# The last query pair as seven block products, early output sums in the wait, and split LayerNorm statistics, in a two-layer linear-attention and gated-MLP kernel

## The chip, the cores and the metric

The kernel runs on one core of one Trainium2 chip. The metric is the time on the device in microseconds (us). All runs that the comparisons below use are in the fast state, at a granted TensorE clock of 1.00 wherever a profile shows it.

## The reference, cut to what matters

```python
q, k, v = split(layernorm(x) @ wqkv)          # 2048 tokens, 1024 wide, 32 heads of 32
pq, pk = phi(q), phi(k)                       # phi(t) = t + 1 if t > 0 else exp(t), plus 1e-6
kv = einsum("bhsd,bhse->bhde", pk, v)
z = sum of pk over the tokens
o = (pq @ kv) / (pq . z + 1e-6)
x = x + o @ wo                                # block A
x = x + ((layernorm(x) @ w_gate) * (layernorm(x) @ w_up)) @ w_down    # block B
# A, B, A, B with the same weights
```

## The kernel before

Block A passes through four stages. First, the projections. Most of them are **quads**: two tiles of 128 tokens, and both halves of the output columns, by a Strassen-Winograd scheme of seven block products (28 matmuls of 512 columns where plain projections take 32). Then the kernel sums over the tokens (`g_part`, `kvt`), a mask keeps the diagonal blocks of heads, and these are multiplied with `wo` (`wprod`). This gives one matrix `wp`. Last comes the output loop, `x + xnT @ wp`, tile by tile. VectorE makes the LayerNorm statistics of the next block in between.

Between the sum and the output loop there is a chain: last `kvt` on TensorE, mask on VectorE, `wprod` on TensorE, evacuation (finished sums are copied out of a **bank**, one of the buffers of PSUM, `ps` in the profile, that the matmuls fill), output. Before the change, two query tiles were held back from the quads to fill it with plain projections:

```python
items += [("k", 6), ("k", 7), ("q", 6)]            # the quad ("q", 7) is missing
...
ph = proj("q", *held[0])            # 8 matmuls each
kvt(2 * KT - 1)
ph()
proj("q", *held[1])()
for g in range(4, 8):
    wprod(g, [0, 4, 1, 3][g - 4], g % 2 == 0)
proj("q", *held[2])()
for g in range(4, 8):
    wprod(NG + g, [0, 2, 1, 3][g - 4], g % 2 == 0)
proj("q", *held[3])()
```

The quads of layer two carry the LayerNorm statistics of the last four tiles, each in one piece:

```python
job(n, 0, lnp.flush_b)
if n % 2:
    job(n, 2, lnp.flush_a)          # two bn_stats and one aggregate, on VectorE
```

And at the end of the output loop of layer one, this work on VectorE prepares block B.

```python
if first and i >= 14:
    prep_s(i - 14)                  # four weight sums of a gate or up unit
...
if nxt.t_next >= 8 and RG["tq"] is None:
    RG["tq"] = t_ops(0)             # block differences; the first reads transposed tiles up to 7
for _ in range(2 if i > 12 else 1):
    if RG["tq"]:
        RG["tq"].pop(0)()
```

Of the kernel before, what the change touches and what calls it, by code (L numbers as in the profile page):

```python
# [180 lines left out]
def build_kernel(nc, A_x, A_wqkv, A_wo, B_w_gate, B_w_up, B_w_down, out):  # L181
    _, S, D = A_x.shape
    F = B_w_gate.shape[1]
    NST, NSB, KT, NG, NFT, NDH = S // 128, S // 512, D // 128, D // 128, F // 128, D // 512
# [8 lines left out]
    NHOLD = 2  # L193
# [52 lines left out]
    O_WP = RA  # L246
# [79 lines left out]
    with ExitStack() as es:  # L326
# [56 lines left out]
        def psb(b):  # L383
            return ps[:, b, :]
# [5 lines left out]
        B_TP = 3  # L390
        B_G = [0, 4]
        B_KVT = [1, 2]
        B_Z = [5, 6]
        B_YY = [5, 6, 7, 3]
        B_GX = [0, 1]
        B_GY = [2, 3]
# [12 lines left out]
        def R(o, n):  # L409
            return [(o, o + n)]  # L410

        def r_x(i, lo=0, hi=D):
            return [(O_X + (i * D + lo) * 2, O_X + (i * D + hi) * 2)]
# [7 lines left out]
        def r_xT(s0, s1):  # L421
            return _seg(O_XT, KT, S * 2, s0 * 2, s1 * 2)

        def r_w(base, lo, hi):
            return _seg(base, KT, D * 2, lo * 2, hi * 2)
# [22 lines left out]

        ln_cnt = [0]

        def ln_a(i, mid=None):
            j = ln_cnt[0] % 8
            ln_cnt[0] += 1
            for h in range(2):
                P.add("dve", (lambda h: lambda e: e.bn_stats(st[j][:, 6 * h:6 * h + 6], x_res[:, i, (D // 2) * h:(D // 2) * (h + 1)]))(h),  # L455
                      rd=r_x(i, (D // 2) * h, (D // 2) * (h + 1)), wr=R(O_ST[j] + 24 * h, 24))
                if mid and h == 0:
                    mid()
            P.add("dve", lambda e: e.bn_aggr(mv[j][:, 0:2], st[j]), rd=R(O_ST[j], 48), wr=R(O_MV[j], 8))
            P.add("pool", lambda e: e.tensor_scalar(out=mv[j][:, 2:3], in0=mv[j][:, 1:2], scalar1=EPS_LN, scalar2=None, op0=ALU.add),  # L460
                  rd=R(O_MV[j] + 4, 4), wr=R(O_MV[j] + 8, 4))
            ln_rstd(j)
            return j
# [36 lines left out]
        class LN:  # L500

            def __init__(self, to, order):
                self.to = to
                self.order = order
                self.q_b = []
                self.q_s = []
                self.q_n = []
                self.q_t = []
                self.n = 0
                self.t_next = 0  # L510
                self.use_dma = False
                self.on_act = False

# [110 lines left out]
                    self.b1_one()  # L624
                    self.b2_one()

            def flush_a(self):
                if self.n < NST and self.pending_ab() < 3:
                    self.start(self.n)

            def flush_step(self):
                self.step_t(1)
# [277 lines left out]
        def layer_A(lnp, nxt, first):  # L910
# [46 lines left out]
            class Quad:  # L957
                n = 0

                def __init__(self, kind, p):  # L960
                    n = Quad.n
                    Quad.n += 1
                    self.kind, self.p = kind, p
                    self.X, self.Z, self.Y = QX[n % 2], QZ[n % 2], QY[(n + NPL) % 3]
                    self.u2 = (u2sb[n % 2], R(O_U2[n % 2], 2048))
                    self.u3 = (u3sb, R(O_U3, 2048))
                    self.i, self.i2 = tok[2 * p], tok[2 * p + 1]
# [208 lines left out]
            for p in range(npr, 6):  # L1176
                items += [("k", p), ("q", p)]
            if npr < 8:
                items += [("k", 6), ("k", 7), ("q", 6)]
            jobs = {}  # L1180

            def job(n, j, f):
                jobs.setdefault((n, j), []).append(f)
# [9 lines left out]
            for n, (kind, p) in enumerate(items):  # L1193
                if kind == "k" and n:
                    sm = s_make(tok, p)
                    job(n - 1, 1, lambda p=p: lnp.need(2 * p + 1))
                    job(n - 1, 1, sm[0])
                    job(n - 1, 2, sm[1])
                    job(n - 1, 3, sm[2])
                    job(n, 1, sm[3])  # L1200
                if kind == "k" and not first:
                    for t in (tok[2 * p], tok[2 * p + 1]):
                        job(n, 0, lambda t=t: dma(xrt[t], nscr[t * 128:(t + 1) * 128, :], r_xr(t), KNL[t], rd=R(V_XN + t * 32, 32)))
                if first:
                    i = NPL + len(LNX) + n
                    for j in range(2):
                        if i < NST:
                            job(n, 2 * j, lambda i=i, j=j: lnstep(i, j))
                    c, m = 9 - max(NPL - 3, 0), len(items)
                    if (n + 1) * c // m > n * c // m:  # L1210
                        job(n, 3, pack)
                elif n >= 2:
                    if n == 9:
                        job(n, 0, lambda: rl.update(o=O_XN[0]))
                    job(n, 0, lnp.flush_b)
                    if n % 2:
                        job(n, 2, lnp.flush_a)

            if items:
                job(len(items) - 1, 3, lambda: load_v(0))  # L1220
# [5 lines left out]
                g_part(0, j)  # L1226

            QL = [Quad(kind, p) for kind, p in items]
            held = [(tok[i], h) for i in range(NST - NHOLD, NST) for h in range(2)]

            def g_part(n, j):
                h, jj = n // KT, n % KT
# [55 lines left out]
            def wprod(n, bank, on_act):  # L1288
# [7 lines left out]
                else:  # L1296
                    P.add("dve", lambda e: e.tensor_scalar(out=dst, in0=psb(bank), scalar1=rz[:, g:g + 1], scalar2=None, op0=ALU.mult),
                          prd=[bank], rd=R(O_RZ, 32), wr=wr)

            for n in range(2 * KT):  # L1300
                if n:
                    gchunk(n)
                if first and n % 2 == 0:
                    pack()
                if n == 2:
                    z_final()
                if n == 4:
                    z_col()
                if n >= 1:
                    kvt(n - 1)  # L1310
                if n >= KT + 2:
                    m = n - KT - 2
                    for d in range(2):
                        if m < 4:
                            wprod(d * NG + m, B_Z[d], True)
                if n >= 2 and na[0] < NNORM:
                    norm(tok[na[0]])
                    na[0] += 1
            ph = proj("q", *held[0])
            kvt(2 * KT - 1)  # L1320
            ph()
            proj("q", *held[1])()
            for g in range(4, 8):
                wprod(g, [0, 4, 1, 3][g - 4], g % 2 == 0)
            proj("q", *held[2])()
            for g in range(4, 8):
                wprod(NG + g, [0, 2, 1, 3][g - 4], g % 2 == 0)
            proj("q", *held[3])()

            def y_seed(n):  # L1330
                if n < NST:
                    xs, bank = x_res[:, tok[n], 512:1024], B_YY[(2 * n + 1) % 4]
                    P.add("act", lambda e: e.copy(psb(bank), xs), rd=r_x(tok[n], 512, 1024), pwr=[bank])

            def y_grp(i, dh, n):
                bank = B_YY[(2 * n + dh) % 4]

                def fn(e):
                    return [e.matmul(psb(bank), xnT[:, g, i * 128:(i + 1) * 128], wp[:, g, dh * 512:(dh + 1) * 512],  # L1339
                                     start=(dh == 0 and g == 0), stop=(g == NG - 1), skip_group_check=True) for g in range(NG)]  # L1340
                xs = x_res[:, i, dh * 512:(dh + 1) * 512]
                rx = r_x(i, dh * 512, (dh + 1) * 512)
                P.add("pe", fn, rd=r_xT(i * 128, (i + 1) * 128) + r_w(O_WP, dh * 512, (dh + 1) * 512), pwr=[bank])
                if dh == 0:
                    P.add("dve", lambda e: e.tensor_tensor(out=xs, in0=psb(bank), in1=xs, op=ALU.add), prd=[bank], rd=rx, wr=rx)
                    return
                P.add("act", lambda e: e.copy(xs, psb(bank)), prd=[bank], wr=rx)

            nxt.use_dma = True
            nxt.on_act = YACT  # L1350
            ring_begin(first)
            for _ in range(3):
                ring_issue()
            y_seed(0)
            for i in range(NST):
                if na[0] < NST:
                    if i % 3 == 2:
                        norm(tok[na[0]])
                        na[0] += 1
                elif RG["n"] < NR:  # L1360
                    ring_issue()
                if first and i % 3 == 1:
                    pack()
                nxt.step_t(1)
                nxt.b1_one()
                if 2 <= i < 15:
                    nxt.start(i - 2)
                y_grp(tok[i], 0, i)
                y_seed(i + 1)
                if i < 15:  # L1370
                    nxt.b2_one()
                y_grp(tok[i], 1, i)
                if first and i >= 14:
                    prep_s(i - 14)
                if not first and i >= 8:
                    stash(i - 8)
                if nxt.t_next >= 8 and RG["tq"] is None:
                    RG["tq"] = t_ops(0)
# [3 lines that stand above are left out]
# [691 lines left out]
```

## Time and profile before

| | before |
|---|---|
| median of 3 runs | 1428.89 us (1428.35 to 1429.38) |
| span of the profiled run | 1426.4 us |
| TensorE busy | 99% |
| VectorE busy | 84% |
| ScalarE busy | 51% |

The prediction below shows the lines of the page and of the timeline and how they are read. Two more lines of the page, on the quads: line, engine, operation, shapes, count, then busy us and mean ns, then idle time before.

```profile
L976 PE MATMUL ps<-arena 128*128 128x512 f16 (+1 forms) x605 | 134.0, 379 | 1.2 <-ACT arena L983 0.6
...
L976 PEld LDWEIGHTS ps<-arena 128*128 128x128 f16 x616 | 59.3, 98 | 74.8 <-ACT arena L983 5.9
```

616 is 22 quads of 28; the trace lacks eleven matmul records of these. So a **stop** of TensorE is measured here from the starts of successive matmuls, less 216 ns (less 110 ns for 256 columns, 56 ns for 128), and not from busy time. These are the steps in the trace of before where nothing holds TensorE up: 215 or 216 ns from start to start at 512 columns, 109 or 110 at 256, 55 or 56 at 128.

### The profile page before, as it was taken

What the parts mean: (1) busy time and instruction counts of PE and PEld (TensorE: products, weight loads), DVE (VectorE), ACT (ScalarE), POOL (GpSimd) and SP (SyncE); (2) the same over time, 40 slices, a digit from 0 to 9 for tenths busy, and PEclk for the clock granted to TensorE, in tenths of its full rate; (3) what the DMA queues carried; (4) which work ended last, traced back from release to release, by engine and by line L of the source; (5) the groups of instructions that cost most, each with busy time, mean ns of one, the idle gap of its engine ahead of it and who ended that gap; (6) DMA issues with size and microseconds to landing.
All of it is one profiled execution on the core that took longest, in us unless ns stands there. A gap on an engine that the chain in (4) does not pass through costs nothing.

```text
span 1426.4 us, 21923 instructions
## 1 busy us (share of the span) xinstructions
PE 1417.6 (99%) x8150; PEld 791.0 (55%) x8209; DVE 1200.9 (84%) x2344; ACT 722.0 (51%) x1471; POOL 153.8 (11%) x197
## 2 busy tenths in 40 slices
PE   9999999999999999999999999999999999999999
PEld 4444444555546566664554444456666475666548
DVE  7897978999978799987689978788888877888888
ACT  5882355444420266655377814567776105777400
POOL 3203521000010000002010045310000100000000
PEclk9999999999999999999999999999999999999999
DMA  7868978997786777768884367767775966777553
GB/s 240 218 141 225 216 179 197 310 311 265 252 264 212 234 254 249 252 228 295 239 281 104 92 177 162 172 196 254 258 246 194 329 221 230 259 258 260 191 205 122
DMA packets 270699, 320.74 MB, mean 225 GB/s; under 512 B 164096, under 2 KB 211072, under 8 KB 270592
## 3 DMA queue, kind: packets, MB, share of 16 engines
q1 hardware_dynamic: 270592, 319.34, 73.2%
q8 instruction: 64, 1.05, 0.3%
q14 instruction: 43, 0.35, 0.1%
HBM read 236.45 MB, written 73.40 MB: 217 GB/s over the span
## 4 chain that ended last, share of the span: by engine, by line
PE 92%; DVE 4%; ACT 2%; issue 1%; DMA 1%; POOL 0%; SPq 0%; DVEq 0%
PE ps L1421 29%; PE ps L1504 17%; PE ps L1853 16%; PE ps L1339 8%; PE ps L1237 8%; PE ps L976 8%; PE ps L1760 5%; DVE arena L808 1%; PE ps L949 1%; DVE arena L811 1%; DVE arena L455 1%; ACT arena L668 1%; DMA arena<-in_A_wqkv_dram 1%; PE ps L1263 1%; PE ps L1290 0%
## 5 line engine op out<-in xcount | busy, mean ns | idle before, releaser
L808 DVE TENSOR_TENSOR arena<-arena 128x512 f16<-128x512 f16 (+7 forms) x1027 | 507.3, 522 | 56.9 <-ACT arena L1508 32.7
L1421 PE MATMUL ps<-arena 128*128 128x512 f16 x1888 | 456.8, 379 | 0.1
L811 DVE SCALAR_TENSOR_TENSOR arena<-ps,arena 128x512 f16<-128x512 f32 (+3 forms) x558 | 358.6, 658 | 86.9 <-PE ps L1853 45.0
L1504 PE MATMUL ps<-arena 128*128 128x256 f16 x2184 | 287.5, 273 | 0.1
L1421 PEld LDWEIGHTS ps<-arena 128*128 128x128 f16 (+1 forms) x1888 | 182.9, 98 | 162.4 <-ACT ps L1450 3.8
L1504 PEld LDWEIGHTS ps<-arena 128*128 128x128 f16 (+1 forms) x2184 | 212.3, 98 | 90.4 <-ACT arena L1508 7.2
L1853 PE MATMUL ps<-arena 128*128 128x512 bf16 (+1 forms) x1048 | 230.6, 379 | 0.8
L1853 PEld LDWEIGHTS ps<-arena 128*128 128x128 f16 x1064 | 104.1, 98 | 123.8
L1426 ACT ACTIVATE arena<-ps 128x512 f32<-128x512 f32 x224 | 133.9, 598 | 76.7 <-PE ps L1421 62.5
L1508 ACT ACTIVATE arena<-ps 128x256 f32<-128x256 f32 x351 | 125.1, 384 | 26.4 <-PE ps L1504 21.5
L976 PE MATMUL ps<-arena 128*128 128x512 f16 (+1 forms) x605 | 134.0, 379 | 1.2 <-ACT arena L983 0.6
L1237 PE MATMUL ps<-arena 128*128 128x512 bf16 x498 | 114.7, 379 | 0.7
L1339 PE MATMUL ps<-arena 128*128 128x512 bf16 x502 | 110.3, 379 | 0.5
L1514 ACT COPY ps<-ps 128x256 f32<-128x256 f32 x182 | 66.3, 364 | 75.5 <-DVE arena L811 28.5
L976 PEld LDWEIGHTS ps<-arena 128*128 128x128 f16 x616 | 59.3, 98 | 74.8 <-ACT arena L983 5.9
L1760 PE MATMUL ps<-arena 128*128 128x256 f16 (+1 forms) x882 | 97.0, 273 | 0.0
L1450 ACT COPY ps<-ps 128x512 f32<-128x512 f32 x112 | 65.4, 583 | 61.5 <-PE ps L1421 51.3
L1078 POOL TENSOR_TENSOR arena<-arena 128x1024 f16<-128x1024 f32 x32 | 77.2, 2413 | 155.7 <-DVE arena L1076 140.8
L1760 PEld LDWEIGHTS ps<-arena 128*128 128x128 f16 x882 | 86.2, 98 | 11.0 <-DVE arena L811 0.2
L1517 DVE TENSOR_TENSOR ps<-ps,arena 128x256 f32<-128x256 f32 x182 | 76.7, 428 | 10.7 <-PE ps L1504 9.5
L1339 PEld LDWEIGHTS ps<-arena 128*128 128x128 f16 x512 | 50.1, 98 | 60.4
L1788 ACT COPY arena<-ps 128x256 f32<-128x256 f32 x8 | 3.0, 373 | 155.8 <-PE ps L1760 155.8
(72 smaller groups left out, 981.0 us busy)
## 6 DMA issues: line engine op xcount, KB each, us to landing
arena<-w_scratch SPq DMA_DIRECT2D x84, 896.0 KB, 4.6
arena<-t_scratch SPq DMA_DIRECT2D x32, 896.0 KB, 5.9
arena<-in_B_w_down_dram SPq DMA_DIRECT2D x24, 896.0 KB, 5.0
arena<-sp_scratch SPq DMA_DIRECT2D x26, 768.0 KB, 4.2
w_scratch<-arena SPq DMA_DIRECT2D x28, 512.0 KB, 6.1
arena<-w_scratch SPq DMA_DIRECT2D x28, 384.0 KB, 4.7
x_scratch<-arena SPq DMA_DIRECT2D x40, 256.0 KB, 5.1
arena<-x_scratch SPq DMA_DIRECT2D x40, 256.0 KB, 4.1
```

Source lines behind the costliest of these rows:

```text
L808: P.add("dve", lambda e: e.tensor_tensor(out=out, in0=a, in1=b, op=op), rd=rd, wr=wr, prd=prd)
L811: P.add("dve", lambda e: e.scalar_tensor_tensor(out=out, in0=a, scalar=sc, in1=b, op0=ALU.mult, op1=op1), rd=rd, wr=wr, prd=prd)
L976: P.add("pe", lambda e: [e.matmul(psb(bank), a[0][:, k, :], b[0][:, k, :], start=(q in (1, 5) and k == 0), stop=(k == 3), skip_group_check ...
L1078: P.add("pool", lambda e: e.tensor_tensor(out=asb[b].rearrange("p (h c) -> p h c", c=32), in0=pbuf.rearrange("p (h c) -> p h c", c=32), in ...
L1237: return [e.matmul(psb(bank), xrt[t][:, jj * 128:(jj + 1) * 128], pk[:, h, t, :], start=(t == tok[0]), stop=(t == tok[NST - 1])) for t in ts]
L1339: return [e.matmul(psb(bank), xnT[:, g, i * 128:(i + 1) * 128], wp[:, g, dh * 512:(dh + 1) * 512], start=(dh == 0 and g == 0), stop=(g == ...
L1421: P.add("pe", lambda e: [e.matmul(psb(bank), w[:, k, :], x[:, k, :], start=(start and k == 0), stop=(k == 3), skip_group_check=True) for k ...
L1426: P.add("act", lambda e: e.activation(t, psb(bank), AF.Copy, scale=SG), prd=[bank], wr=r)
L1504: P.add("pe", lambda e: [e.matmul(psb(bank)[:, 256 * half:256 * half + 256], w[:, k, :], xx[:, k, :], start=(start and k == 0), stop=(k == ...
L1508: P.add("act", lambda e: e.activation(d, src, AF.Copy, scale=sc), prd=[xk], wr=rd_)
L1760: P.add("pe", lambda e: [e.matmul(psb(bank)[:, 256 * half:256 * half + 256], a[:, k, 128 * r:128 * r + 128], b[:, k, :], start=(start and ...
L1853: P.add("pe", lambda e: [e.matmul(psb(bank), hv[:, 7 * hf + k, t * 128:(t + 1) * 128], w[:, k, :], start=(q in "15" and hf == 0 and k == 0 ...
```

## The change

The intent is four matmuls fewer per layer. The last query pair becomes a quad. The wait is filled with the first halves of the output sums of tiles 0 and 1, whose `wp` blocks 0 to 3 are ready by then. The statistics are split into two halves in successive quads. Cut to the core:

```diff
-        B_Z = [5, 6]
+        B_Z = [5, 3]
...
-                    self.X, self.Z, self.Y = QX[n % 2], QZ[n % 2], QY[(n + NPL) % 3]
+                    self.X, self.Z, self.Y = QX[n % 2], QZ[n % 2], QY[(n + NPL + 2) % 3]
...
-                items += [("k", 6), ("k", 7), ("q", 6)]
+                items += [("k", 6), ("k", 7), ("q", 6), ("q", 7)]
...
-                    if n % 2:
-                        job(n, 2, lnp.flush_a)
+                    job(n, 2 if n % 2 == 0 else 0, lambda k=int(n % 2 != 0): lnp.flush_a(k))
...
+            y_part(0, 0, 0)
+            y_part(0, 1, 0)
+            kvt(2 * KT - 1)
+            y_part(1, 0, 0)
+            for g in range(4, 8):
+                wprod(g, [0, 1, 4, 2][g - 4], g % 2 == 0)
+            y_part(1, 1, 0)
+            for g in range(4, 8):
+                wprod(NG + g, [0, 1, 4, 2][g - 4], g % 2 == 0)
```

Each `y_part` is four matmuls. The residual of tiles 0 and 1 is copied into their second output bank one step before the last sum (`y_seed`). The four `proj("q", ...)` are gone.

More of the change, by code (lines that the diff above doesn't have):

```diff
@@ L449, in build_kernel, with ln_a @@
         ln_cnt = [0]
-        def ln_a(i, mid=None):
-            j = ln_cnt[0] % 8
-            ln_cnt[0] += 1
-            for h in range(2):
+        def ln_a(i, mid=None, rest=False):
+            if rest:
+                j = (ln_cnt[0] - 1) % 8
+            else:
+                j = ln_cnt[0] % 8
+                ln_cnt[0] += 1
+            for h in range(rest, 2):
                 P.add("dve", (lambda h: lambda e: e.bn_stats(st[j][:, 6 * h:6 * h + 6], x_res[:, i, (D // 2) * h:(D // 2) * (h + 1)]))(h),
                       rd=r_x(i, (D // 2) * h, (D // 2) * (h + 1)), wr=R(O_ST[j] + 24 * h, 24))
+                if mid == "half":
+                    return
                 if mid and h == 0:
@@ L510, in __init__ @@
                 self.t_next = 0
+                self.open = False
                 self.use_dma = False
@@ L625, in flush_b, with flush_a @@
                     self.b2_one()
-            def flush_a(self):
-                if self.n < NST and self.pending_ab() < 3:
-                    self.start(self.n)
+            def flush_a(self, k):
+                if k:
+                    if self.open:
+                        self.q_b.append((self.n, ln_a(self.order[self.n], None, True)))
+                        self.n += 1
+                        self.open = False
+                elif self.n < NST and self.pending_ab() < 3:
+                    ln_a(self.order[self.n], "half")
+                    self.open = True
             def flush_step(self):
@@ L1228, in layer_A @@
             QL = [Quad(kind, p) for kind, p in items]
-            held = [(tok[i], h) for i in range(NST - NHOLD, NST) for h in range(2)]
             def g_part(n, j):
@@ L1298, in wprod, with y_seed @@
                           prd=[bank], rd=R(O_RZ, 32), wr=wr)
+            def y_seed(n):
+                if n < NST:
+                    xs, bank = x_res[:, tok[n], 512:1024], B_YY[(2 * n + 1) % 4]
+                    P.add("act", lambda e: e.copy(psb(bank), xs), rd=r_x(tok[n], 512, 1024), pwr=[bank])
             for n in range(2 * KT):
+                if n == 2 * KT - 1:
+                    y_seed(0)
+                    y_seed(1)
                 if n:
@@ L1318, in layer_A, with y_mm, y_part @@
                     na[0] += 1
-            ph = proj("q", *held[0])
-            kvt(2 * KT - 1)
-            ph()
-            proj("q", *held[1])()
-            for g in range(4, 8):
-                wprod(g, [0, 4, 1, 3][g - 4], g % 2 == 0)
-            proj("q", *held[2])()
-            for g in range(4, 8):
-                wprod(NG + g, [0, 2, 1, 3][g - 4], g % 2 == 0)
-            proj("q", *held[3])()
-            def y_seed(n):
-                if n < NST:
-                    xs, bank = x_res[:, tok[n], 512:1024], B_YY[(2 * n + 1) % 4]
-                    P.add("act", lambda e: e.copy(psb(bank), xs), rd=r_x(tok[n], 512, 1024), pwr=[bank])
+            def y_mm(n, dh, gs):
+                i, bank = tok[n], B_YY[(2 * n + dh) % 4]
+                P.add("pe", lambda e: [e.matmul(psb(bank), xnT[:, g, i * 128:(i + 1) * 128], wp[:, g, dh * 512:(dh + 1) * 512],
+                                                start=(dh == 0 and g == 0), stop=(g == NG - 1), skip_group_check=True) for g in gs],
+                      rd=r_xT(i * 128, (i + 1) * 128)[gs[0]:gs[-1] + 1] + r_w(O_WP, dh * 512, (dh + 1) * 512)[gs[0]:gs[-1] + 1], pwr=[bank])
+            def y_part(n, dh, k):
+                y_mm(n, dh, range(4 * k, 4 * k + 4))
             def y_grp(i, dh, n):
                 bank = B_YY[(2 * n + dh) % 4]
-                def fn(e):
-                    return [e.matmul(psb(bank), xnT[:, g, i * 128:(i + 1) * 128], wp[:, g, dh * 512:(dh + 1) * 512],
-                                     start=(dh == 0 and g == 0), stop=(g == NG - 1), skip_group_check=True) for g in range(NG)]
+                if n < 2:
+                    y_part(n, dh, 1)
+                else:
+                    y_mm(n, dh, range(NG))
                 xs = x_res[:, i, dh * 512:(dh + 1) * 512]
                 rx = r_x(i, dh * 512, (dh + 1) * 512)
-                P.add("pe", fn, rd=r_xT(i * 128, (i + 1) * 128) + r_w(O_WP, dh * 512, (dh + 1) * 512), pwr=[bank])
                 if dh == 0:
@@ L1353, in layer_A @@
                 ring_issue()
-            y_seed(0)
             for i in range(NST):
@@ L1367, in layer_A @@
                     nxt.start(i - 2)
-                y_grp(tok[i], 0, i)
-                y_seed(i + 1)
+                if i != 1:
+                    y_grp(tok[i], 0, i)
+                if i == 0:
+                    y_grp(tok[1], 0, 1)
+                else:
+                    y_seed(i + 1)
                 if i < 15:
```

## The prediction

> **What bounds the kernel now.** I read the page first (busy shares, the row of slices, the chain that ended last), then the timeline of TensorE, then the waits before it.
>
> ```profile
> PE 1417.6 (99%) x8150; PEld 791.0 (55%) x8209; DVE 1200.9 (84%) x2344; ACT 722.0 (51%) x1471; POOL 153.8 (11%) x197
> PE 92%; DVE 4%; ACT 2%; issue 1%; DMA 1%; POOL 0%; SPq 0%; DVEq 0%
> ```
>
> TensorE (PE) is busy for 99% of the span and makes up 92% of the chain. A busy TensorE need not be a dense one, so I compared start times. A matmul of 512 columns is drawn 379 ns long, but its successor starts long before that. The wait between the summing over tokens (L1237, L1263) and the output (L1339) in layer two, on the timeline of TensorE:
>
> ```profile
> 878.38 0.39 PE L1263 MATMUL ps<-arena 128*128 128x128 bf16 x4
> 878.60 1.89 PE L949 MATMUL ps<-arena 128*128 128x512 bf16 x8
> 880.33 0.39 PE L1263 MATMUL ps<-arena 128*128 128x128 bf16 x4
> 880.55 1.89 PE L949 MATMUL ps<-arena 128*128 128x512 bf16 x8
> 882.28 1.03 PE L1290 MATMUL ps<-arena 128*128 128x512 bf16 x4
> ...
> 884.87 1.03 PE L1290 MATMUL ps<-arena 128*128 128x512 bf16 x4
> 885.73 1.89 PE L949 MATMUL ps<-arena 128*128 128x512 bf16 x8
> 887.46 7.72 PE L1339 MATMUL ps<-arena 128*128 128x512 bf16 x34
> ```
>
> Columns: start, duration, line, shapes, count. L949 are the plain projections of the last two query tiles, held back to fill this wait. Eight of them take 880.33 - 878.60 = 1.73 us, that is 216 ns each. From 878.60 to 887.46 nothing is lost: 32 matmuls of L949, four small ones and eight of L1290 make 6.91 + 0.22 + 1.73 = 8.86 us, which is the stretch. Layer one shows the same from 169.44 to 178.30.
>
> Where is TensorE not dense? I took the starts of successive matmuls over the whole timeline, subtracted 216 ns (110 for 256 columns), and allowed for missing records. Beside the start of the kernel (3.7 us in the first 20 us, untouched here) only one stretch loses time that adds up: the block-product quads of layer two, three stops of 0.35, 0.36 and 0.37 us near 765, 771 and 784, in all 1.08 us. The waits before TensorE name ScalarE (ACT); its own waits name VectorE (DVE), which shows no idle time there at all:
>
> ```profile
> 760.04 1.42 DVE L455 BATCH_NORM_STATS2 arena<-arena 128x6 f32<-128x512 bf16 x2
> 761.50 0.21 DVE L459 BATCH_NORM_AGGREGATE arena<-arena 128x2 f32<-128x12 f32 x1
> 761.62 0.37 DVE L808 TENSOR_TENSOR arena<-arena 128x512 f16<-128x512 f16 x1
> 761.91 0.68 DVE L996 SCALAR_TENSOR_TENSOR arena<-ps,arena 128x512 f16<-128x512 f32 x1
> 762.63 0.72 ACT L1002 ACTIVATE arena<-arena 128x512 bf16<-128x512 f16 x1 [1.06 <-DVE arena L996]
> 764.85 0.57 ACT L983 COPY arena<-ps 128x512 f32<-128x512 f32 x1
> 765.47 2.76 PE L976 MATMUL ps<-arena 128*128 128x512 f16 x12 [0.19 <-ACT arena L983]
> ```
>
> A whole LayerNorm statistic (1.57 us from its start to the next VectorE instruction) stands ahead of L996, for which ScalarE waits, and the ScalarE copy that releases the next matmul comes late. The same statistic returns at 760.04, 772.52 and 785.01, so two quads take 12.48 us where 56 matmuls at 216 ns need 12.10: VectorE is the bound there, by 0.38 us a pair.
>
> [...] the mask step of the wait (L1268, operand in PSUM) and each half of the statistics measure 692 and 691 ns, so 0.69 us is used for both. [...] L996 starts only after the statistics queued ahead of it. [...]
>
> **The change, part by part.**
>
> 1. Seven products for the last query pair. Removed per layer: 4 x 8 = 32 matmuls of L949. Added: one quad, 7 x 4 = 28 of L976. Four fewer at 216 ns make 0.86 us a layer, 1.73 us for both. All of it is on the chain. The operands exist already, since the key pair 7 uses the same token sums. On VectorE the held projections took 4 x (0.28 + 0.69) us; a query quad without LayerNorm takes some 4.9 to 5.5 us of its 6.05 (windows over the last quads of layers one and two), so it fits behind TensorE. The PSUM rotation is shifted by two so that the last quad still uses bank 2; the first quad of layer two now uses bank 2 for Y, whose VectorE reader ends at 725.55, before the second product starts at 726.41.
>
> 2. Output sums begun in the wait. Of the four output groups of tiles 0 and 1, the first half (16 matmuls) moves forward. It adds nothing: 3.45 us out of the output loop and into the wait. The question is whether 16 matmuls cover what 32 did. Eight still stand ahead of the last kvt step, as before, so its ScalarE copy is covered. Behind it stand only four (0.86 us) instead of eight. On the old time axis kvt ends its issue at 880.55, the mask runs on VectorE from 880.75 to 881.44, and a release takes about 0.05 us (ACT copy to matmul above: 765.42 to 765.47), so the weights product may start at 881.49. TensorE arrives at 880.55 + 0.86 = 881.41. A stop of 0.08 us, 0.16 for both layers. The two sets of four weights products are evacuated two by ScalarE (about 0.65 us each) and two by VectorE (0.70). The banks repeat after eight matmuls, 1.73 us, against an evacuation ended about 1.0 us after the first. The last evacuation lands near 885.2; the first group that reads it starts near 885.8. No further stop, with 0.6 us to spare. The seeds are copied near 875 to 876.6, where ScalarE is idle.
>
> 3. Statistics split. VectorE gets no less to do, but the work comes earlier: half behind the keys' quad, half at the head of the next. For the first tile the whole 1.57 us moves to before 746, and there VectorE still has gaps (0.13, 0.34, 0.37 and 0.26 us at 742.6, 744.1, 745.2 and 745.8). They can take 1.1 us. From 746 on VectorE has no idle time in either kernel until about 799, so it runs about 1.1 us ahead of before throughout, against 1.08 us of stops. I count 0.9 us, as some stop may remain behind the second half.
>
> Sum: -1.73 - 0.9 + 0.16 = -2.5 us. 1428.9 - 2.5 = 1426.4 us. A dead load of a block of query weights stays (its reader is gone); it costs queue time only.
>
> **The rivals.** (a) The wait opens: with the filler halved, mask, product and evacuation lie bare. If the mask came late by one VectorE instruction, or the release cost twice as much, each layer would lose 0.3 to 0.7 us more: 1427.0 to 1427.8. For it: the margin in the sum is below zero. Against it: VectorE is idle for 2.12 us before the mask in layer two and 1.38 in layer one. (b) VectorE stays the bound in the quads: the excess of 0.38 us a pair is work, not order, and a split cannot remove it. Then only part 1 remains, less the 0.16: 1427.3. For it: the saturation from 746 to 799. Against it: the gaps before 746 and after 799, which can take the excess of three pairs (1.1 us). (c) The output loop turns VectorE-bound, since tiles 0 and 1 no longer give it 6.9 us of easy start: norms of the last two tiles and the next LayerNorm now come at once. In that loop VectorE is busy 43.8 of 55.5 us (layer one) and 42.4 of 55.4 (layer two), so it has room; it would cost up to 1 us. (d) The saving is hidden by a transfer: no DMA wait stands before TensorE after the first 20 us, so there is none to uncover.
>
> **Range and chances.** The matmul count (1.73 us) is certain; the split is worth 0 to 1.1, the new stop costs 0.1 to 1.4. That gives 1426.1 to 1428.5 at the corners, most of the weight near 1426.4. The three runs of before span 1.0 us, so half a microsecond of noise is added below: 1425.5 to 1427.6. A change of 2% would be 29 us, more than ten times all that is moved: faster 0.005, same 0.99, slower 0.005.
>
> **What would show it.** In the profile after: 28 more L976-type matmuls and no projection matmuls in the wait of each layer; the quads of layer two ending with no stop of 0.3 us near 765, 771 and 784; statistics singly, 0.69 us each; a stop of 0.1 us at most before the second-half weights products; no idle TensorE at the head of the output loop; a span of about 1424.0. Stops of 0.3 us or more ahead of the weights products would make it rival (a), unchanged stops in the quads rival (b), gaps inside the output loop (c). A time above 1428 means that the new wait ate the saved matmuls.

The sum came to -1.73 - 0.9 + 0.16 = -2.5 us, all worked out from starts, gaps and durations in the profile of before, and the 0.69 us of the mask step stands as measured there (691 to 693 ns, L1268).

## The result

| | before | after |
|---|---|---|
| median, this set of runs (4 each) | 1429.14 us | 1426.10 us (1425.64 to 1426.57) |
| ratio of the means | | 0.9979, interval 0.9962 to 0.9996 |
| span of the profiled run | 1426.4 us | 1423.9 us |

A ratio is the mean time of one kernel's fast runs over that of the other's of the same rounds, so not quite the ratio of the medians quoted. A second set of five runs gave 1426.45 against 1428.85 us, ratio 0.9982. So the change is worth 2.4 to 3.0 us of 1429.

The page of the changed kernel, first the span and busy shares and the chain's engines, then the two lines of the quads:

```profile
span 1423.9 us, 21979 instructions
...
PE 1418.7 (100%) x8201; PEld 790.9 (56%) x8201; DVE 1199.1 (84%) x2348; ACT 727.0 (51%) x1481; POOL 154.7 (11%) x197
...
PE 95%; DVE 2%; DMA 1%; issue 1%; POOL 0%; SPq 0%; ACT 0%; DVEq 0%; ACTq 0%
...
L988 PE MATMUL ps<-arena 128*128 128x512 f16 (+1 forms) x672 | 146.2, 379 | 0.0
...
L988 PEld LDWEIGHTS ps<-arena 128*128 128x128 f16 x672 | 65.3, 98 | 79.8 <-ACT arena L995 4.3
```

L976 is now L988: 672 is two more quads of 28, one per layer. The idle time of TensorE before them, 1.2 us in all, is now zero. The wait of layer two on the timeline of TensorE (start, duration, line, shapes, count; L1273 is `kvt`, L1300 is `wprod`, L1339 the output):

```profile
882.95 0.39 PE L1273 MATMUL ps<-arena 128*128 128x128 bf16 x4
883.17 1.89 PE L1339 MATMUL ps<-arena 128*128 128x512 bf16 x8
884.90 0.39 PE L1273 MATMUL ps<-arena 128*128 128x128 bf16 x4
885.12 1.03 PE L1339 MATMUL ps<-arena 128*128 128x512 bf16 x4
886.07 1.04 PE L1300 MATMUL ps<-arena 128*128 128x512 bf16 x4
886.95 1.03 PE L1339 MATMUL ps<-arena 128*128 128x512 bf16 x4
```

The four matmuls at 885.12 need 0.86 us and could be followed at 885.98; the first `wprod` starts at 886.07. This is the predicted stop: 84 ns here, 86 ns in layer one. Nothing else in the wait loses time.

The quads of layer two, the whole run of them on TensorE and then the first split statistic on VectorE (L458 and L464):

```profile
725.04 95.18 PE L988 MATMUL ps<-arena 128*128 128x512 bf16 x440
...
740.81 0.69 DVE L458 BATCH_NORM_STATS2 arena<-arena 128x6 f32<-128x512 bf16 x1
741.41 0.68 DVE L1008 SCALAR_TENSOR_TENSOR arena<-ps,arena 128x512 f16<-128x512 f32 x1
...
743.71 0.69 DVE L458 BATCH_NORM_STATS2 arena<-arena 128x6 f32<-128x512 bf16 x1
744.44 0.21 DVE L464 BATCH_NORM_AGGREGATE arena<-arena 128x2 f32<-128x12 f32 x1
```

The profile draws 440 matmuls as one block: their starts are 440 x 216 ns = 95.0 us, and the last one lasts 0.16 us beyond its step. No stop is left of the three of before (0.35, 0.36 and 0.37 us). The statistic that stood at 747.1 to 748.7 before now stands, in halves, at 740.8 and 743.7.

One stop is new in this profile, and the prediction did not have it. At the head of the gate and up products of layer one, TensorE waits for VectorE. The changed kernel, TensorE, then the VectorE instruction that will matter:

```profile
232.52 7.93 PE L1445 MATMUL ps<-arena 128*128 128x512 f16 x36
241.03 4.49 PE L1445 MATMUL ps<-arena 128*128 128x512 f16 x20 [0.57 <-DVE arena L823]
...
220.75 1.23 DVE L820 TENSOR_TENSOR arena<-arena 128x2048 f16<-128x2048 f16 x1 [2.87 <-DMA arena<-arena]
```

and the same two places before:

```profile
233.55 12.26 PE L1421 MATMUL ps<-arena 128*128 128x512 f16 x56
...
221.03 1.22 DVE L808 TENSOR_TENSOR arena<-arena 128x2048 f16<-128x2048 f16 x1 [2.13 <-DMA arena<-arena]
```

36 matmuls take 7.78 us, so the next could start at 240.30; it starts at 241.03, a stop of 0.73 us. Before, 56 run without a break. In both, VectorE waits over 2 us for a DMA (2.87 and 2.13 us): the block difference `t_ops` reads tile 7, whose transpose, itself a DMA, has not landed, that is, its data has not arrived.

One small stop has gone that nobody aimed at: 0.25 us near 1318 us, in the last gate and up products. All four profiles with layer two's old structure have it at that place (before, and later b_again, e2 and e5), none of the ten with the new one; there ScalarE, for which the next products wait, had been late (in b_again the weight load of L1504 waits 0.58 us for L1508). Why was not pursued.

The sum of what the two traces show is -1.73 (eight matmuls) - 1.08 (stops in the quads) + 0.17 (two stops in the wait) - 0.25 (the stop near 1318) + 0.73 (the new stop) = -2.16 us. With 0.25 us less until the first quad begins this makes -2.4 us, against -2.5 us in the spans. That last term is scatter of the start of the kernel: over the fourteen profiles the first quad begins anywhere from 65.27 to 66.05 us.

So there are two questions for the chip. Are the parts worth what the traces say? And did layer one's saving, 0.78 us, run into a VectorE-bound place and get lost?

### The profile page after: what moved, and what is told of

Its sections match the earlier page's. It is cut to its first block, busy times and chain, and to the rows that moved or that the text cites. A ratio compares the mean times of both kernels' runs of the same rounds, so it can differ in the third digit from the quotient of the medians.

```text
span 1423.9 us, 21979 instructions
## 1 busy us (share of the span) xinstructions
PE 1418.7 (100%) x8201; PEld 790.9 (56%) x8201; DVE 1199.1 (84%) x2348; ACT 727.0 (51%) x1481; POOL 154.7 (11%) x197
## 4 chain that ended last, share of the span: by engine, by line
PE 95%; DVE 2%; DMA 1%; issue 1%; POOL 0%; SPq 0%; ACT 0%; DVEq 0%; ACTq 0%
PE ps L1445 28%; PE ps L1528 17%; PE ps L1877 16%; PE ps L988 10%; PE ps L1247 8%; PE ps L1784 7%; PE ps L1339 4%; PE ps L961 3%; DMA arena<-arena 1%; DVE arena L458 1%; PE ps L1273 1%; DVE arena L820 1%; PE ps L1300 0%; DMA arena<-in_A_wqkv_dram 0%; SPq L428 0%
## 5 line engine op out<-in xcount | busy, mean ns | idle before, releaser
L820 DVE TENSOR_TENSOR arena<-arena 128x512 f16<-128x512 f16 (+9 forms) x1035 | 510.3, 521 | 58.5 <-ACT arena L1532 32.8
L1877 PEld LDWEIGHTS ps<-arena 128*128 128x128 f16 x1064 | 104.1, 98 | 123.8
L988 PE MATMUL ps<-arena 128*128 128x512 f16 (+1 forms) x672 | 146.2, 379 | 0.0
L1247 PE MATMUL ps<-arena 128*128 128x512 bf16 x512 | 116.1, 379 | 0.0
L1339 PE MATMUL ps<-arena 128*128 128x512 bf16 x512 | 111.8, 379 | 0.0
L988 PEld LDWEIGHTS ps<-arena 128*128 128x128 f16 x672 | 65.3, 98 | 79.8 <-ACT arena L995 4.3
L1784 PEld LDWEIGHTS ps<-arena 128*128 128x128 f16 x882 | 86.2, 98 | 11.0 <-DVE arena L823 0.2
L1339 PEld LDWEIGHTS ps<-arena 128*128 128x128 f16 x512 | 49.9, 98 | 59.5
```

The source lines that it names most:

```text
L820: P.add("dve", lambda e: e.tensor_tensor(out=out, in0=a, in1=b, op=op), rd=rd, wr=wr, prd=prd)
L988: P.add("pe", lambda e: [e.matmul(psb(bank), a[0][:, k, :], b[0][:, k, :], start=(q in (1, 5) and k == 0), stop=(k == 3), skip_group_check ...
L1247: return [e.matmul(psb(bank), xrt[t][:, jj * 128:(jj + 1) * 128], pk[:, h, t, :], start=(t == tok[0]), stop=(t == tok[NST - 1])) for t in ts]
L1339: P.add("pe", lambda e: [e.matmul(psb(bank), xnT[:, g, i * 128:(i + 1) * 128], wp[:, g, dh * 512:(dh + 1) * 512], start=(dh == 0 and g == ...
L1784: P.add("pe", lambda e: [e.matmul(psb(bank)[:, 256 * half:256 * half + 256], a[:, k, 128 * r:128 * r + 128], b[:, k, :], start=(start and ...
L1877: P.add("pe", lambda e: [e.matmul(psb(bank), hv[:, 7 * hf + k, t * 128:(t + 1) * 128], w[:, k, :], start=(q in "15" and hf == 0 and k == 0 ...
```

## The experiments

Twelve runs were made, two of them repeats of the given kernels, each with five timed executions, one of them profiled; all gave the correct result. "Change" is the median against that of the kernel before in the same set of runs; the ratio is of means.

| run | median us | change | ratio, interval | stop at the gate head |
|---|---|---|---|---|
| e1_no_split | 1427.04 | -1.87 | 0.9988, 0.9975 to 1.0000 | 0.75 |
| e2_split_only | 1428.17 | -0.74 | 0.9993, 0.9980 to 1.0006 | 0.71 |
| e3_layer2_only | 1426.50 | -2.41 | 0.9982, 0.9970 to 0.9995 | 0.39 |
| e4_prep_early | 1425.47 | -3.44 | 0.9976, 0.9962 to 0.9990 | 0 |
| b_again | 1429.31 | +0.46 | 1.0002, 0.9988 to 1.0015 | 0.60 |
| a_again | 1426.45 | -2.40 | 0.9982, 0.9969 to 0.9994 | 0.30 |
| e5_before_prep | 1428.15 | -0.70 | 0.9995, 0.9982 to 1.0007 | 0 (0.25 in the loop) |
| e8_prep_fill | 1425.48 | -3.37 | 0.9976, 0.9963 to 0.9988 | 0 (0.50 in the loop) |
| e6_wait_open | 1427.53 | -1.40 | 0.9991, 0.9978 to 1.0003 | 0.50 |
| e7_no_dead_load | 1426.82 | -2.11 | 0.9984, 0.9971 to 0.9998 | 1.10 |
| e9_late_t | 1425.37 | -3.56 | 0.9974, 0.9962 to 0.9987 | 0 |
| e10_late_t_layer2 | 1426.14 | -2.94 | 0.9982, 0.9968 to 0.9995 | 0 |

The kernel before against itself (b_again) shows what the clock can tell: its interval is 1.3 thousandths to either side, and its median is 0.46 us off. Differences below half a microsecond are read from traces only.

### e1_no_split: the statistics in one piece again

```diff
-                    job(n, 2 if n % 2 == 0 else 0, lambda k=int(n % 2 != 0): lnp.flush_a(k))
+                    if n % 2:
+                        job(n, 2, lambda: (lnp.flush_a(0), lnp.flush_a(1)))
```

> The changed kernel with the statistics of layer two in one piece again, as before. Theory (the split let VectorE run 1.1 us ahead and so removed the three stops of TensorE in the quads of layer two): the three stops come back near 764, 771 and 783 us, 1.0 to 1.1 us in all; the span is about 1.0 us above the changed kernel's, near 1425.0, the time 1.8 to 2.1 us below before. Rival (the stops went because the quads, the PSUM banks or the phase changed, not because of the split): no stops, the time equals the changed kernel's, about 3.0 us below before.

The timeline of TensorE shows the three stops again:

```profile
765.71 6.22 PE L988 MATMUL ps<-arena 128*128 128x512 f16 x27 [0.19 <-ACT arena L995]
772.13 12.28 PE L988 MATMUL ps<-arena 128*128 128x512 f16 x55 [0.20 <-ACT arena L995]
784.60 5.57 PE L988 MATMUL ps<-arena 128*128 128x512 f16 x25 [0.20 <-ACT arena L995]
```

By starts they are 0.35, 0.36 and 0.36 us, 1.08 in all (the 0.19 or 0.20 printed is less, since the drawn end of a matmul lies 0.16 us past its step). The time is 1.87 us below before, as expected, and near the sum of the trace without the split: -1.73 + 0.17 - 0.25 = -1.81. The new quads and banks do not remove the stops, the split does.

### e2_split_only: the kernel before with the split alone

The edit is the `ln_a`, `flush_a` and `job` lines of the change in the kernel before.

> The kernel before with the split of the statistics alone. Theory: the stops in the quads of layer two go, the time is 1.0 to 1.1 us below before (ratio 0.9993); everything else as before. Rival (the split needs the rest of the change): the stops stay and the ratio is 1.0000.

The stops in the quads went: no break in the run of L976 matmuls. The median fell 0.74 us, with an interval that includes zero, so the clock alone would not settle it. The surprise stood elsewhere: layer one of this kernel is that of before, and it had a stop of 0.71 us at the gate head. So that stop is not a mark of the change.

### e3_layer2_only: layer one as before

The edit makes the quad list, the banks and the filler of the wait depend on the layer; the old code runs in layer one.

> The changed kernel, but layer one as before (four plain projections in the wait, no output sums begun early); layer two with the whole change. Theory (what layer one saves, 0.78 us, is mostly given back at the head of the gate and up products, where TensorE then waits for VectorE, 0.6 to 0.7 us near 240 us): no such wait there, and the time lies only 0.1 to 0.3 us above the changed kernel's. Rival (the wait near 240 us is a chance of the profiled run, layer one saves its 0.78 us): 0.8 us above the changed kernel's.

The time was 2.41 us below before, within 0.1 us of a_again and 0.6 us of the first set of the changed kernel. Taken alone this supports "layer one's saving is given back". But this run had a stop of 0.39 us where the theory said none, and the stretch from the first quad to the first gate product took 168.03 us, as before, against 167.25 in the changed kernel: the saving of 0.78 us is there in the trace. The theory as I had put it fell; what was left was that the stop varies.

### b_again and a_again: both kernels once more

> The kernel before once more, against itself: ratio 1.0000, the width of its interval is what the timing can tell apart. Its profile is a second look at the stop near 241 us, which the profile of before did not show but that of its twin with split statistics did (0.71 us, with layer one untouched). Theory A (the stop depends on when a transposed tile lands, which varies from run to run: the stop is 12.3 us less the time from VectorE's release by that landing to the end of the output loop of layer one): 0 to 0.75 us in this run, obeying that sum. Theory B (the change gives layer one's saving back there): 0 in the kernel before, always.

> The changed kernel once more, for a second profile and for more runs: ratio 0.9979 (3.0 us). Theory A: the stop near 240 us lies anywhere from 0 to 0.75 us and again equals 12.3 us less the lead. Theory B: 0.7 us again, whatever the lead.

The kernel before in its second profile, TensorE and then the VectorE instruction after the landing:

```profile
233.34 7.93 PE L1421 MATMUL ps<-arena 128*128 128x512 f16 x36
241.71 4.49 PE L1421 MATMUL ps<-arena 128*128 128x512 f16 x20 [0.44 <-DVE arena L811]
...
221.43 1.23 DVE L808 TENSOR_TENSOR arena<-arena 128x2048 f16<-128x2048 f16 x1 [2.74 <-DMA arena<-arena]
```

It has a stop of 0.60 us that its first profile did not have. Let the **lead** be the time from the start of that VectorE instruction to the first gate product (233.34 - 221.43 = 11.91 us here). Over all profiles with `t_ops` and `prep_s` in their old places:

| run | lead us | 12.51 - lead | measured stop us |
|---|---|---|---|
| before | 12.52 | -0.01 | 0 |
| a_again | 12.21 | 0.30 | 0.30 |
| e3_layer2_only | 12.13 | 0.38 | 0.39 |
| e6_wait_open | 12.02 | 0.49 | 0.50 |
| b_again | 11.91 | 0.60 | 0.60 |
| e2_split_only | 11.82 | 0.69 | 0.71 |
| e1_no_split | 11.78 | 0.73 | 0.75 |
| after | 11.77 | 0.74 | 0.73 |
| e7_no_dead_load | 11.42 | 1.09 | 1.10 |

(The expectations count the lead to the last output matmul, 0.22 us earlier, hence their 12.3.) From the start of that VectorE instruction to the moment when TensorE goes on, 20.3 us pass (221.43 to 241.71 above), and in all this time VectorE has no pause over 0.05 us. The 36 products that need not wait for it cover 7.8 us; the lead has to cover the other 12.5. The stop is what it leaves uncovered. The constant 12.51 is fitted to the table; what the table shows is that one constant fits nine profiles to 0.02 us. The stop occurs in both kernels: 0, 0.60, 0.71 and 0.39 us in the four with layer one as before, 0.73, 0.30, 0.75 and 1.10 us in the four with the changed layer one (without e6). The means, 0.4 and 0.7, lie too close for four samples of this scatter.

### e4_prep_early, e5_before_prep and e8_prep_fill: less work behind the landing

e4 is the changed kernel, e5 the kernel before, with this edit:

```diff
-                if first and i >= 14:
-                    prep_s(i - 14)
+                if first and i in (11, 12):
+                    prep_s(i - 11)
```

> The changed kernel with the eight weight sums of the first two gate and up units made at tiles 11 and 12 of the output loop of layer one instead of at 14 and 15, where VectorE sits idle for 4.6 us in all. Theory (VectorE waits up to 2.9 us for a transposed tile near 218 to 221 us, is then never idle until 250, and TensorE of the changed kernel runs into it at 240): the stop near 240 us goes, and the time is 0.5 to 0.7 us below the changed kernel's. Rival (the stop comes from the landing of something else, such as a DMA, at a fixed time): the stop stays or moves, no gain.

> The kernel before with the eight weight sums at tiles 11 and 12 of layer one's output loop instead of 14 and 15. Theory A: VectorE is free 1.6 to 3 us sooner, no stop near 241 us, the time 0.2 to 0.7 us below before, as the stop is taken away in the runs of before that have it. Theory B: nothing to win, ratio 1.0000.

e8 adds a fifth covering matmul to e4: `y_mm(1, 1, range(1))` ahead of the first `wprod`, and `range(1, 4)` in place of the four between the sets.

> The changed kernel with the eight weight sums at tiles 11 and 12, and one more of the early output matmuls moved ahead of the first four weights products (five cover the mask instead of four, three the second set). The stop of 0.09 us before the weights products goes in both layers, no new stop appears before the second set; with the sums 0.6 to 0.9 us below the changed kernel, 1425.0 to 1425.5. If the release and not the mask sets that stop, it stays at 0.09.

The stop at the gate head is gone in all three. The medians are 3.44, 0.70 and 3.37 us below before (the interval of e5 includes zero). The fifth matmul did what it should: the stop of 0.09 us is gone in both layers (the products follow their predecessor in steps of 216 ns). But in e5 and e8 a new stop of 0.25 and 0.50 us stands inside the output loop, in e8 here:

```profile
230.03 3.63 PE L1339 MATMUL ps<-arena 128*128 128x512 bf16 x16 [0.34 <-DVE arena L1356]
```

L1356 is VectorE's evacuation of an output bank. VectorE still stood before `t_ops` for 1.85 us, until the tile landed at 221.65 us, and the evacuations queued behind it came late (the next one started at 224.48). Moving other work away had in these two only moved the place where the landing is paid. The same sum holds with a smaller constant: without their own stops the leads of e4, e5 and e8 are 11.93, 11.61 and 11.35 us, and the stops in the loop are 0, 0.25 and 0.50 us, which is what each lacks to 11.86.

### e6_wait_open: the cover of the mask taken away

```diff
             kvt(2 * KT - 1)
-            y_part(1, 0, 0)
             for g in range(4, 8):
...
                 wprod(NG + g, [0, 1, 4, 2][g - 4], g % 2 == 0)
+            y_part(1, 0, 0)
```

> The changed kernel with the four early output matmuls that stand between the last kvt step and the first weights products moved behind both sets of products: the same work, the wait left bare. Theory (those four cover the mask and leave 0.09 us open): the stop before the weights products becomes 0.09 + 0.86 = 0.95 us in each layer, in all 1.7 us more; in layer one up to 0.7 us of it may come back where TensorE would otherwise have waited at the head of the gate and up products, so the time is 1.1 to 1.7 us above the changed kernel's. Rival (the cover does not matter, as the products wait for something else): no change.

The timeline of TensorE in layer two:

```profile
885.91 0.39 PE L1273 MATMUL ps<-arena 128*128 128x128 bf16 x4
887.08 1.04 PE L1300 MATMUL ps<-arena 128*128 128x512 bf16 x4 [0.79 <-DVE arena L1278]
```

From the last `kvt` (four steps of 0.056 us, to 886.13) to the product at 887.08 are 0.95 us in both layers, where four matmuls had left 0.09. The time is 1.0 to 1.6 us above the two sets of the changed kernel. So the four matmuls do cover 0.86 us each time, and the mask is what the products wait for.

### e7_no_dead_load: the unread load removed

The edit deletes the line that loads `wq[:, 0:4, 512:1024]` after the quads.

> The changed kernel without the load of a block of query weights that nothing reads any more. Theory (queue time only): time equal to the changed kernel's within the noise of 0.3 us. Rival (the load delays the transposed tiles on their queue, so that they land sooner without it): the stop near 240 us goes and the time falls by up to 0.7 us.

No gain: 2.11 us below before, and in its profile the tile landed later than in any other (lead 11.42, stop 1.10 us). So nothing shows that this load holds the landing back.

The traces show where the variation comes from, one step further back. The transposes are issued one after another by a queue on SyncE (SP). Three that stand in it shortly before tile 7's, in the kernel before and in e7, the runs of the longest and the shortest lead:

```profile
208.03 5.84 SPq L579 DMA_TRANSPOSE arena<-arena  x3
...
207.46 6.80 SPq L585 DMA_TRANSPOSE arena<-arena  x3
```

Of these, issuing the first took 3.11 and 4.07 us. In all nine profiles of the table that issue ended 0.80 to 0.88 us after the landing of a weight load (`arena<-w_scratch`) that stands before it in the queue. Counted from the first gate product, this landing varies by 0.81 us, and the later it is, the shorter is the lead (correlation 0.92). Tile 7's own transpose lands 2.09 to 2.24 us after the end of its issue each time. So most of the lateness is there before that transpose is issued. This is read from traces; no run tested it, and why the weight load varies stays open.

### e9_late_t: do not queue VectorE behind a landing

The changed kernel with e8's fifth matmul and

```diff
-                if first and i >= 14:
-                    prep_s(i - 14)
+                if first and i in (10, 11):
+                    prep_s(i - 10)
...
-                if nxt.t_next >= 8 and RG["tq"] is None:
+                if nxt.t_next >= 8 + first and RG["tq"] is None:
```

> The changed kernel with one more early output matmul ahead of the weights products, the eight weight sums at tiles 10 and 11 of layer one's output loop, and its four block differences of transposed tiles begun one tile later, so that VectorE no longer stands before an operation whose tile has not landed while finished output banks wait behind it. Theory (the in-order wait for the landing costs the stop, at the head of gate and up or, with the sums moved alone, inside the output loop): no stop of TensorE over 0.1 us from the quads of layer one to the end of its gate and up products, whatever the landing; time 0.5 to 0.9 us below the changed kernel, 1425.0 to 1425.6. Rival (VectorE is simply full there): a stop of 0.2 us or more remains somewhere between 215 and 245 us.

TensorE at the gate head, and the first block difference on VectorE:

```profile
232.63 12.25 PE L1446 MATMUL ps<-arena 128*128 128x512 f16 x56
...
221.89 1.22 DVE L820 TENSOR_TENSOR arena<-arena 128x2048 f16<-128x2048 f16 x1
```

The difference starts at about the same time as ever (221.89), but without a DMA wait, and everything that had been stuck behind it is done. From the first quad of layer one to the end of its gate and up products there is one stop above 0.1 us, 0.2 us near 67 us, which lies ahead of all this and which the profiles of both kernels have. Median 1425.37 us, 3.56 below before: the lowest of all, and lower than both given kernels, although over the changed kernel alone (0.5 to 1.2 us by medians) the two intervals overlap. The medians of e4 and e8 lie within 0.2 us, so the clock does not show that e9 beats them.

### e10_late_t_layer2: is layer one's saving real?

This is e9 with e3's condition, so layer one has the old quads and the old wait, and no stop that could hide a difference.

> The kernel of the previous run (late tile differences, early weight sums, five covering matmuls) with layer one's quads and wait as before the change; layer two whole. The landing can no longer stop TensorE, so what layer one saves has nowhere to hide. Theory A (the 0.78 us of layer one is real and was blurred by the varying stop): the stretch from the first quad to the first gate product is 0.87 us longer than in the previous run, 168.0 against 167.2 us, no stop near 241 us, and the time 0.6 to 1.1 us above it, 1426.0 to 1426.5. Theory B (layer one's saving is lost whatever is done): the time equals the previous run's, 1425.4.

From the first quad to the first gate product it takes 168.03 us, e9 167.17: 0.86 us more. The time is 1426.14, 0.77 us above e9's (0.62 by their changes against before), though from another set of runs on another chip, and the intervals overlap. So it is the traces that show layer one's saving to be real, and to arrive in full once nothing downstream varies; the clock agrees.

## Why the prediction was right

The time on record was 1426.4 us (1425.5 to 1427.6); measured were 1426.10 and 1426.45. By its steps:

- **Four matmuls fewer a layer, 1.73 us.** Right. The page counts 672 for 616, the projections in the wait are gone, and e10 against e9, neither of which has a stop in that wait, shows 0.86 us for layer one.
- **The wait: a stop of 0.08 us, no other.** Right: 0.086 and 0.084 us. e6 and e8 show that the cover is short by just this much: four matmuls less open it to 0.95 us, one more closes it; the trace of e6 names the mask (L1278) as what the products wait for. Rival (a) did not come about.
- **The split: 0.9 us of 1.08.** The mechanism was right (VectorE gets ahead by filling gaps before 746 us, with no less work to do: from 741.0 to 745.8 it is busy for 4.66 of 4.80 us, before for 3.63, and both profiles have 86 half statistics), the size a little low: all 1.08 us went. The term that was mis-sized is "some stop may remain behind the second half"; none did. e1 brings back the stops alone, e2 removes them alone. Rival (b) fell. After the change, the next gap of over 0.2 us on VectorE ends at 793.3 in the profiled run, where before it ended at 799.7.
- **The transfer, rival (d): "no DMA wait stands before TensorE after the first 20 us, so there is none to uncover".** This step failed. The premise is true, the conclusion not. A DMA wait of 2.13 us stood before VectorE in the profile I had read, at 221 us, and a late landing reached TensorE 20.3 us later through VectorE's queue (b_again). In the profile of before the lead was 12.52 us, just enough for no stop, so nothing showed. It did not spoil the forecast, because the kernel before pays it as well in other runs.
- **The output loop, rival (c).** The loop itself had no stop after the change, as predicted from its 79% busy VectorE. But an average over the loop did not show that its last third, from 221 us on, and the head of the gate products are full. The bound that I looked for exists, at its edge.

That the forecast of -2.5 us equals the difference of the profiled spans is in part luck. The three terms that it had measure -2.64 us together; the three that it did not have, +0.73 (the stop at the gate head), -0.25 (the stop near 1318) and -0.25 (the start), nearly cancel.

Some figures of the prediction are a little off. Its list of stops before the change leaves out the 0.25 us near 1318, 0.21 us near 67 and two of 0.20 us near 953 and 1194 (these three are in the profiles of both kernels). The evacuations that it puts at 0.65 and 0.70 us take 0.69 and 0.74 (L1295, L1297), which its 0.6 us to spare covered. Its corners come to 1426.2 and 1428.6 when added again, and the range ends 1 us below the upper one.

What stays open: why the weight load ahead of the transposes, and with it the landing of tile 7, varies (the lead by 1.1 us), and whether it is on average later with the changed layer one; also the stop near 1318 us, 0.25 us of gain that the prediction did not have and no run explains (e7 has one of 0.24 us near 1042 instead). The difference between the gain of 3.0 us in the first set and 2.4 in the second may be such scatter; no run shows it.

## What to carry to other kernels

When the main engine is full, count its instructions and check the few places where work moves off its cover: here each step could be forecast to a tenth of a microsecond from starts in the trace. Look for DMA waits before every engine, not only before the bound engine: here a wait of 2.13 us (before) to 3.23 us (e7) stood before VectorE, the work queued behind it came late, and TensorE stopped for up to 1.10 us. Compare the slack behind such a wait with how much the landing varies from run to run (here the lead, by 1.1 us). One profile shows one landing; put work that is ready ahead of an operation that waits for a transfer.
